# Attention's matmuls in one array tiling of 64x32 tiles, with two score buffers: four transformer layers on one core

## The chip, the core and the metric

The kernel runs on one core of a Trainium2 chip. Its engines work in parallel, each with its own queue of instructions, and wait for each other through semaphores: PE (TensorE, matrix products; its weight loads are shown apart as PEld), DVE (VectorE), ACT (ScalarE), POOL (GpSimd) and SP (SyncE, which here only issues DMAs). Matrix products go from SBUF into PSUM, whose eight banks of 128 partitions x 2 KB (512 float32 values a partition) are read by DVE and ACT. The metric is the device time of one execution in microseconds, the median of several runs.

## The reference

Four layers in a row on x of 2048 rows by 512 columns, A, B, A, B; each is `x = x + layer(layernorm(x))`. Both have 32 heads of 16 columns.

```python
def A(x, wqkv, wo):
    q, k, v = split_heads(x @ wqkv)
    p = softmax(einsum("bhqd,bhkd->bhqk", q, k) * Dh ** -0.5)
    return merge(einsum("bhqk,bhkd->bhqd", p, v)) @ wo
...
def B(x, wqkv, w_phi, wo):
    q, k, v = split_heads(x @ wqkv)
    pq, pk = q @ w_phi, k @ w_phi
    phi_q = concat(softmax(pq), softmax(-pq))
    phi_k = concat(softmax(pk), softmax(-pk))
    num = phi_q @ (phi_k.T @ v)
    den = phi_q @ sum(phi_k) + 1e-6
    return merge(num / den) @ wo
```

## The kernel before

**The softmax attention of a layer A** is one loop of 512 steps (`attention`, line 1005). Heads go in octets `o` of eight, octets in two groups `g` of four heads; a step is one (g, j, kt): four heads, a block `j` of 512 queries and a tile `kt` of 128 keys. In a step:

- `scores` (line 911) makes two score tiles ("halves") of 128 keys x 2 heads x 512 queries, each in a buffer of two PSUM banks, one head a bank. An operand has 49 rows: 16 of the high part and 32 of the low parts of float16 pairs, one of them the row of the shift. Two heads lie at partitions 0 and 64, so a half is two matmuls in row tiles of 64 (printed 49*128 in the trace). ACT reads both banks of a half at once with one exponential (line 919, 128x1024) into a float32 tile `p`.
- `pvs` (line 922) multiplies the `p` of two steps earlier (`LAG = 2`) with the values: four heads in four column tiles of 32 (128*32), each over all 128 keys, summed over the 16 tiles `kt` in one PSUM bank, tag "PV". Float32 operands take two passes. At `kt == 15` the bank holds the numerators and denominators of one block of queries; `norm` (line 533) transposes it with DVE into a tile `yt` and divides. A *turn* is the change of this accumulator, every 16 steps, 32 times a layer.
- then *pieces* of side work: projections of the next octet's q and k (`project`, line 677) and values (`values`, line 686), squares and norms, and, late in the layer, the output projection (`o_block`, line 572). A piece of a projection is `mm_cols` (line 613): four matmuls in column tiles of 32. Twelve pieces make a 128x512 result in a PSUM bank of tag "M". DVE then evacuates it: three operations for q and k (lines 792 to 794: scale and clamp from PSUM, round to float16, remainder), a transpose for values, from which 16 small DMAs on SP's queue carry the tile `vyt` to its place, one scale-and-add for the output projection (line 605). `yt`, `vyt` and `tq` share a tag of three buffers.

What orders it: PE's order is the written one (`manual_schedule` for PE), scores of both halves, PV, pieces; the other engines are ordered by the scheduler. Pieces are dealt by a credit that grows 1.33 to 1.55 a step, by a table of rates; one to three pieces a step, at least two at a turn:

```python
credit = min(credit + rate(n), 6)
least = 2 if turn else 0
most = 3
```

PSUM's eight banks are three score buffers of two banks (`psS`), and one bank each for tags "PV" and "M" (`ps1`). Outside attention the two lone banks alternate, and the three doubles serve projections, transposes and layer B. Layer B (`feed`, line 1090, and `finish`) runs block by block after the attention, with its key-value sums in one double buffer throughout. `p` tiles have six buffers.

## Time and profile before

| | us |
|---|---|
| median of the runs | 2531.31 (2529.28 to 2533.78) |
| span of the profiled execution | 2531.0 |
| first softmax attention, from its first to its last exponential | 72.5 to 1023.0 |
| second softmax attention | 1331.0 to 2279.5 |
| PE busy | 2431.7 (96%) |
| ACT busy | 2172.7 (86%), of which 1888.0 in the 2048 exponentials of line 919 |
| DVE busy | 976.1 (39%) |
| POOL busy | 381.8 (15%) |

One execution is profiled, and its instructions are grouped by line, engine, operation and tile. In a row of a group, `x2048` counts instructions, then follow their busy time in us and the mean ns of one, and behind the bar the idle time of the engine just ahead of them with the instruction that ended most of it. `49*128` or `128*32` behind a matmul is the tile of the array that it uses (rows x columns). In a row of the timeline the first number is the start in us from the span's start, the second the time until the last of the run of like instructions ends; `[0.84 <-PE s L916]` is the idle time ahead of them and what ended it. Matmul ends are modelled, so times are taken from start to start where that can be done. The granted PE clock was 1.00 in both attentions.

### The profile page before, as it was taken

The page shows a single profiled execution, that of the slowest core. Times are in us where ns is not written, and L with a number is a line of the kernel's source. Part 1 is how long each engine was busy: PE and PEld are TensorE (multiplying, and loading weights), DVE is VectorE, ACT ScalarE, POOL GpSimd, SP SyncE. Part 2 cuts the span into 40 slices and gives each one's busy share as a digit, 9 for nine tenths or more (in the row PEclk, how much of TensorE's full clock was granted, in tenths as well). Part 3 has the DMA queues.
Part 4 walks back from the last instruction along what each step waited for, and adds up shares of the span by engine and source line. Part 5 has one row for each costly group of instructions (what it writes and reads, how often), then busy time and mean ns, then how long its engine had stood idle before and what let it go on. Part 6 is the DMA issues. An engine that isn't in the chain of part 4 may idle for free.

```text
span 2531.0 us, 51504 instructions
## 1 busy us (share of the span) xinstructions
PE 2431.7 (96%) x21346; PEld 749.7 (30%) x21346; DVE 976.1 (39%) x1900; ACT 2172.7 (86%) x2429; POOL 381.8 (15%) x507
## 2 busy tenths in 40 slices
PE   6999999999999999989799999999999999998998
PEld 4222222222232222444352222222222222224543
DVE  8112211212233316989860121112122111458897
ACT  6899999999999999454439999999999999993553
POOL 3001000001000000456430010000010000005552
PEclk9999999999999999999899999999999999999999
DMA  5400320141035412101133003202300351110003
GB/s 196 73 22 6 55 40 2 27 57 58 1 80 145 161 51 76 51 9 34 59 104 49 10 10 50 37 1 47 65 1 14 68 144 38 67 68 26 10 17 110
DMA packets 110846, 135.35 MB, mean 53 GB/s; under 512 B 64024, under 2 KB 65672, under 8 KB 108424
## 3 DMA queue, kind: packets, MB, share of 16 engines
q1 hardware_dynamic: 109416, 129.18, 20.4%
q8 instruction: 169, 2.77, 0.5%
q0 software_dynamic: 1184, 2.77, 0.3%
q14 instruction: 77, 0.63, 0.1%
HBM read 60.06 MB, written 39.85 MB: 39 GB/s over the span
## 4 chain that ended last, share of the span: by engine, by line
PE 77%; DVE 12%; ACT 5%; issue 3%; POOL 2%; DMA 0%; ACTq 0%; POOLq 0%; DVEq 0%; SPq 0%
PE pv L930 37%; PE s L916 21%; PE pqk L617 6%; PE po L617 5%; ACT p L919 3%; DVE su L1173 1%; PE pbv L1103 1%; PE pk L1103 1%; PE pq L1103 1%; DVE f L1165 1%; DVE f L1166 1%; DVE mx L1162 1%; POOL f L1182 1%; DVE st L421 1%; PE pst L478 1%
## 5 line engine op out<-in xcount | busy, mean ns | idle before, releaser
L919 ACT ACTIVATE p<-s 128x1024 f32<-128x1024 f32 x2048 | 1888.0, 1115 | 14.7 <-PE s L916 11.9
L930 PE MATMUL pv<-p,v 128*32 128x512 f32 x8192 | 1093.4, 606 | 2.6 <-DVE yt L535 1.8
L916 PE MATMUL s<-kq 49*128 49x512 f16 x3872 | 607.2, 383 | 11.0 <-DMA kq<-sh 3.4
L916 PEld LDWEIGHTS <-kq 49*128 49x128 f16 x3968 | 138.3, 94 | 632.2 <-issue 620.8
L930 PEld LDWEIGHTS pv<-p,v 128*32 128x32 f32 x8192 | 162.0, 108 | 396.1 <-issue 366.1
L719 POOL TENSOR_TENSOR sq<-stg 128x512 bf16<-128x512 f16 x48 | 69.8, 1455 | 1041.5 <-DVE stg L793 938.5
L535 DVE STREAM_TRANSPOSE yt<-pv 128x512 f32<-128x512 f32 x64 | 45.8, 716 | 453.0 <-PE pv L930 436.4
L792 DVE TENSOR_SCALAR tq<-pqk,c_qk 128x512 f32<-128x512 f32 x48 | 36.0, 749 | 445.1 <-PE pqk L617 445.1
L1182 POOL TENSOR_TENSOR f<-f,su 128x1024 f32<-128x1024 f32 x62 | 119.9, 1934 | 384.6 <-DVE su L1176 352.4
L1103 PEld LDWEIGHTS <-xnTa 128*128 128x128 f16 x1152 | 110.7, 99 | 151.6 <-DVE f L1166 23.6
L617 PEld LDWEIGHTS <-wA 128*32 128x32 f16 (+1 forms) x2496 | 86.0, 97 | 196.7 <-issue 169.3
L605 DVE SCALAR_TENSOR_TENSOR xt<-po,c_oA,xt 128x512 f32<-128x512 f32 x64 | 47.1, 735 | 234.6 <-PE po L617 234.6
L617 PE MATMUL pqk<-xnTb,wA 128*32 128x512 f16 (+1 forms) x1248 | 118.7, 381 | 2.2 <-ACT xnTb L488 2.2
L617 PE MATMUL pqk<-xnT,wA 128*32 128x512 f16 (+1 forms) x1224 | 110.9, 379 | 1.2 <-ACT xnT L488 1.2
L1167 ACT ACTIVATE f<-f,c_pB 128x1024 f32<-128x1024 f32 x64 | 72.7, 1148 | 45.3 <-DVE f L1166 45.2
L1103 PE MATMUL pbv<-wbv,xnTa 128*128 128x512 f16 x384 | 92.9, 394 | 19.0 <-DVE f L1166 19.0
L1188 ACT ACTIVATE fk<-f 128x1024 f16<-128x1024 f32 x30 | 31.7, 1057 | 72.2 <-POOL f L1182 72.2
L617 PE MATMUL po<-woA,ob 128*32 128x512 f16 x1152 | 92.3, 379 | 0.0
L1103 PE MATMUL pq<-wbqk,xnTa 128*128 128x512 f16 x384 | 88.4, 379 | 0.7 <-DVE vt L1130 0.7
L1103 PE MATMUL pk<-wbqk,xnTa 128*128 128x512 f16 x384 | 88.5, 379 | 0.0
L1173 DVE TENSOR_REDUCE su<-f 128x64 f32<-128x1024 f32 x64 | 77.5, 1211 | 9.1 <-ACT f L1167 8.3
L1214 ACT ACTIVATE qT<-pqt 128x512 f32<-128x512 f32 x64 | 34.9, 593 | 49.6 <-PE pqt L1213 49.6
(283 smaller groups left out, 1895.2 us busy)
## 6 DMA issues: line engine op xcount, KB each, us to landing
kq<-stg SPq DMA_DIRECT2D x168, 128.0 KB
xd<-xt SPq DMA_DIRECT2D x40, 512.0 KB
xt<-xd SPq DMA_DIRECT2D x40, 512.0 KB
v<-vyt SPq DMA_DIRECT2D x384, 16.0 KB
oD<-osp SPq DMA_DIRECT2D x24, 256.0 KB
ob<-oD SPq DMA_DIRECT2D x8, 768.0 KB
xt<-in_A_x_dram SPq DMA_DIRECT2D x8, 512.0 KB
wbqk<-dBqk SPq DMA_DIRECT2D x2, 2048.0 KB
```

The lines of the kernel that those rows point to most:

```text
L535: nc.vector.transpose(yt.rearrange("p a b -> p (a b)"), ps)
L605: nc.vector.scalar_tensor_tensor(xt[:, u, :], ps, co, xt[:, u, :], op0=ALU.mult, op1=ALU.add)
L617: nc.tensor.matmul(ps[r, :], w[:, r], x, start=(n == 0), stop=(n == of - 1), skip_group_check=cols)
L719: nc.gpsimd.tensor_tensor(sq, hi, hi, ALU.mult)
L792: nc.vector.tensor_scalar(tq, ps, cqk, CLAMP, op0=ALU.mult, op1=ALU.min)
L916: nc.tensor.matmul(s[:, u, :], self.side(g, half, r, 0, kt * P, P), self.side(g, half, r, 1, j * 512, 512), start=True, stop=True)
L919: nc.scalar.activation(pt, s, AF.Exp, scale=0.25 / (QS * QS))
L930: nc.tensor.matmul(acc[32 * hh:32 * hh + 32, :], self.oct[o]["v"][:, r:r + 32], pt[:, hh % 2, :], start=(kt == 0), stop=(kt == NT - 1), sk ...
L1103: nc.tensor.matmul(dst, xnT[:, a, c, t * P:(t + 1) * P], w(b, c), start=(i == 0 and c == 0), stop=(i == 2 and c == NC4 - 1))
L1167: nc.scalar.activation(f, f, AF.Exp, scale=con["pB"])
L1173: nc.vector.tensor_reduce(su, f[:, r, :], AX.X, ALU.add)
L1182: nc.gpsimd.tensor_tensor(f3, f3, self.part_sums(f3, slice(0, 64), factor), ALU.mult)
```

## The change

All of attention's matmuls use tiles of 64 rows x 32 columns, so that the tiling of the array never changes inside the loop.

- *Scores*: a half is eight matmuls (four column tiles of 32 keys x two heads) in place of two.
- *PV*: for each head two matmuls, over keys 0 to 63 and 64 to 127, into two banks, which is a double buffer (`double`) of its own pool. The two banks are added later.
- *Projections*: `mm_cols` splits the contraction of 128 into halves that go to two banks (`psum_pair`), eight matmuls a piece; the norms' matmuls likewise.
- *Sums of the halves*: for PV and values DVE transposes both banks and POOL adds the two results (`turned_sum`); q and k are evacuated by five DVE operations in place of three; the output projection by two scale-and-adds.
- *PSUM*: two score buffers in place of three; one double for PV; two lone banks of tag "M" in place of "PV" and "M". Outside attention `banks` gives the two score buffers and the double in turn; layer B's key-value sums take the double.
- *Order*: scores of half 0, PV, scores of half 1, pieces. In a step whose PV opens a new accumulator (`turn`, now the step after the last product with the old one) PV comes behind the pieces; the least of two pieces is now in that step.
- The tail's output projection after attention (`cols` only while `state["att"]`) uses the whole array.

```diff
-    psS = pool("psS", bufs=3, space=bass.MemoryType.PSUM)
-    ps1 = pool("ps1", bufs=1, space=bass.MemoryType.PSUM)
+    psS = pool("psS", bufs=2, space=bass.MemoryType.PSUM)
+    psW = pool("psW", bufs=1, space=bass.MemoryType.PSUM)
+    ps1 = pool("ps1", bufs=2, space=bass.MemoryType.PSUM)
...
+    def psum_pair(name):
+        return [psum1(name + str(i)) for i in range(2)]
+    def double():
+        return psW.tile([P, 2, 512], F32, tag="W", name="double")
+    def banks(name):
+        if state["whole"]:
+            state["turn"] = (state["turn"] + 1) % 3
+            if state["turn"] == 0:
+                return double()
+        return psS.tile([P, 2, 512], F32, tag="S", name=name)
...
+    def turned_sum(ps, name):
+        ys = [np_.tile([P, 16, 32], F32, tag="yt", name=name + str(i), bufs=3) for i in range(2)]
+        for y, half in zip(ys, ps):
+            nc.vector.transpose(y.rearrange("p a b -> p (a b)"), half)
+        nc.gpsimd.tensor_tensor(ys[0], ys[0], ys[1], ALU.add)
+        return ys[0]
...
-        yt = np_.tile([P, 16, 32], F32, tag="yt", name="yt", bufs=3)
-        nc.vector.transpose(yt.rearrange("p a b -> p (a b)"), ps)
+        yt = turned_sum(ps, "yt")
...
-                    nc.vector.scalar_tensor_tensor(xt[:, u, :], ps, co, xt[:, u, :], op0=ALU.mult, op1=ALU.add)
+                    for half in ps if cols else (ps,):
+                        nc.vector.scalar_tensor_tensor(xt[:, u, :], half, co, xt[:, u, :], op0=ALU.mult, op1=ALU.add)
...
+        for i in range(4):
+            c = slice(32 * i, 32 * i + 32)
+            for h in range(2):
+                r = slice(64 * h, 64 * h + 64)
+                nc.tensor.matmul(ps[h][c, :], w[r, c], x[r], start=(n == 0), stop=(n == of - 1), skip_group_check=True)
...
-                    nc.vector.tensor_scalar(tq, ps, cqk, CLAMP, op0=ALU.mult, op1=ALU.min)
-                    nc.vector.tensor_scalar(hi, tq, -CLAMP, None, op0=ALU.max)
-                    nc.vector.scalar_tensor_tensor(lo, tq, -CLAMP, hi, op0=ALU.max, op1=ALU.subtract)
+                    nc.vector.tensor_scalar(tq, ps[0], cqk, None, op0=ALU.mult)
+                    nc.vector.scalar_tensor_tensor(tq, ps[1], cqk, tq, op0=ALU.mult, op1=ALU.add)
+                    nc.vector.tensor_scalar(tq, tq, CLAMP, -CLAMP, op0=ALU.min, op1=ALU.max)
+                    nc.vector.tensor_copy(hi, tq)
+                    nc.vector.tensor_tensor(lo, tq, hi, ALU.subtract)
...
+            s = psS.tile([P, 2, 512], F32, tag="S", name="s")
+            for c in range(4):
                 for u in range(2):
...
+                    nc.tensor.matmul(s[32 * c:32 * c + 32, u, :], self.side(g, half, 64 * u, 0, kt * P + 32 * c, 32),
+                                     self.side(g, half, 64 * u, 1, j * 512, 512), start=True, stop=True, skip_group_check=True)
...
-                self.acc = ps1.tile([P, 512], F32, tag="PV", name="pv")
+                pair = double()
+                self.acc = [pair[:, h, :] for h in range(2)]
...
+                for h in range(2):
+                    r = slice(64 * h, 64 * h + 64)
+                    nc.tensor.matmul(acc[h][32 * hh:32 * hh + 32, :], self.oct[o]["v"][r, x:x + 32],
+                                     pt[r, hh % 2, :], start=(kt == 0), stop=(kt == NT - 1), skip_group_check=True)
...
-                    self.scores(g, j, kt)
+                    self.scores(g, j, kt, 0)
                     pend.append((g, j, kt))
-                    turn = False
-                    if len(pend) > LAG:
-                        turn = pend[0][2] == NT - 1
+                    turn = len(pend) > LAG and pend[0][2] == 0
+                    if len(pend) > LAG and not turn:
                         self.pvs(*pend.popleft())
+                    self.scores(g, j, kt, 1)
...
+                    if turn:
+                        self.pvs(*pend.popleft())
```

How instructions move shows at three places. The first is PE in a plain step of the first attention, between the scores of a step's second half and a piece. Names such as `kq_1_981` are tiles with a running number, `kq_0` and `kq_1` the operands of the two halves, `wA` the weights of a projection. Before:

```order
L916 LDWEIGHTS kq_1_981
L916 MATMUL s<-kq_1_981 128x512
L930 MATMUL pv<-p,v_157 32x512 x4
L617 LDWEIGHTS wA
L617 MATMUL pqk<-xnT_3_152,wA 32x512
```

And now, where the scores of half 0 end and those of half 1 begin:

```order
L944 LDWEIGHTS kq_0_593
L944 MATMUL s<-kq_0_593 32x512
L961 MATMUL double<-p,v_160 32x512 x8
L944 LDWEIGHTS kq_1_594
L944 MATMUL s<-kq_1_594 32x512
```

PV, now eight matmuls, has moved from behind both halves to between them, and a score matmul writes 32 keys in place of 128.

The second is PE at a turn of the new kernel: the end of a piece of the values' projection (two banks, `pv_2268` and `pv_2269`), the first PV on the new accumulator, and the next step's first scores.

```order
L642 LDWEIGHTS wAv
L642 MATMUL pv_2268<-xnT_3_155,wAv 32x512
L642 LDWEIGHTS wAv
L642 MATMUL pv_2269<-xnT_3_155,wAv 32x512
L961 MATMUL double<-p,v_160 32x512 x8
L944 LDWEIGHTS kq_0_593
L944 MATMUL s<-kq_0_593 32x512
```

Here PV stands behind the pieces and directly ahead of the next step's scores of half 0.

The third is DVE around a turn in the second octet: an evacuation of q or k (`pqk`) and then `norm` of a finished accumulator. Before:

```order
L792 TENSOR_SCALAR tq<-pqk,c_qk 128x512
L793 TENSOR_SCALAR stg<-tq 128x512
L794 SCALAR_TENSOR_TENSOR stg<-tq,stg 128x512
L535 STREAM_TRANSPOSE yt<-pv 128x512
L537 TENSOR_SCALAR rec<-yt 128x16
L538 RECIPROCAL rec<-rec 128x16
L542 TENSOR_TENSOR yn<-yt,rec 128x16x16
```

And now:

```order
L819 TENSOR_SCALAR tq<-pqk_4630,c_qk 128x512
L820 SCALAR_TENSOR_TENSOR tq<-pqk_4631,c_qk,tq 128x512
L821 TENSOR_SCALAR tq<-tq 128x512
L822 CAST stg<-tq 128x512
L823 TENSOR_TENSOR stg<-tq,stg 128x512
L548 STREAM_TRANSPOSE yt_5174<-double 128x512
L548 STREAM_TRANSPOSE yt_5175<-double 128x512
L555 TENSOR_SCALAR rec<-yt_5174 128x16
L556 RECIPROCAL rec<-rec 128x16
L560 TENSOR_TENSOR yn<-yt_5174,rec 128x16x16
```

Five operations stand ahead of two transposes where three stood ahead of one; between the second transpose and the division POOL's `L549 TENSOR_TENSOR yt_5174<-yt_5174,yt_5175 128x512` makes the sum.

More of the change, by code (lines that the diff above doesn't have):

```diff
@@ L585, in o_block @@
             if wide:
-                ps2 = psS.tile([P, 2, 512], F32, tag="S", name="po2")
+                ps2 = banks("po2")
             if early and t2 == 0:
@@ L629, in v_block @@
         for t2 in range(2):
-            ps = psS.tile([P, 2, 512], F32, tag="S", name="pv_")
+            ps = banks("pv_")
             for u in range(2):
@@ L695, in values @@
                         yield
-            yt = np_.tile([P, 16, 32], F32, tag="yt", name="vyt", bufs=3)
-            nc.vector.transpose(yt.rearrange("p a b -> p (a b)"), ps)
+            yt = turned_sum(ps, "vyt")
             for a in range(4):
@@ L859, in feed_end @@
         def feed_end(self):
-            ps = psS.tile([P, 2, 512], F32, tag="S", name="pqk2")[:, 0, :]
+            ps = banks("pqk2")[:, 0, :]
             run(self.project(0, NJ - 1, ps, 0))
@@ L1092, in feed @@
             if self.kvp is None:
-                self.kvp = psS.tile([P, 2, 512], F32, tag="S", name="kvp")
+                self.kvp = double()
+                state["whole"] = False
             qT = [big([P, 4, 512], F32, f"qT{j}_{i}") for i in range(2)]
@@ L1240, in heads @@
             for k in range(2):
-                ps = [psS.tile([P, 2, 512], F32, tag="S", name="pn") for _ in range(2)]
+                ps = [banks("pn") for _ in range(2)]
                 for g in range(4):
```

75 lines of the change are left out of this document (34 added, 41 removed).

## The prediction

> **What bounds the kernel now.** First the share of each engine by stage (busy time of line 919 alone in four stretches: us, busy us and count, clock, DMA share, GB/s), then the page's groups and its chain, then the timeline of single steps.
>
> ```profile
> core 0: us, ACT busy (x), PEclk, DMA share, GB/s
> 72.50:1023.00 950.50, 944.72 (x1024) 1.00 0.24 56
> 400.00:600.00 200.00, 199.68 (x218) 1.00 0.22 40
> 1331.00:2279.50 948.50, 943.25 (x1024) 1.00 0.20 45
> ```
>
> The first and third stretch are the two softmax attentions: 1899 of the span's 2531.0 us, and each runs 1024 exponentials (two a step, 512 steps). In a quiet stretch 218 of them take 199.68 us: **0.917 us each, 1.83 us a step**. At that cadence one attention lasts 1024 × 0.917 = 939 us; it takes 950.5 and 948.5. So ACT stands still, or gets its scores late, for only 11.5 + 9.5 = 21 us in all. That is all that a faster TensorE could win.
>
> ```profile
> PE 77%; DVE 12%; ACT 5%; issue 3%; POOL 2%; DMA 0%; ACTq 0%; POOLq 0%; DVEq 0%; SPq 0%
> L919 ACT ACTIVATE p<-s 128x1024 f32<-128x1024 f32 x2048 | 1888.0, 1115 | 14.7 <-PE s L916 11.9
> 400.00:600.00 200.00, 199.45 (x1896) 48.19 (x1888) 40.36 (x80) 199.68 (x218) 13.14 (x11) 1.00 0.22 40
> ```
>
> The chain (first row) names PE, which reads as if PE alone set the pace. The last row (PE, PEld, DVE, ACT, POOL busy in 400 to 600 us) shows PE and ACT both full: the side work is dealt out at 1.33 to 1.55 pieces a step, so that PE's step comes out as long as ACT's. One step of PE:
>
> ```profile
> 599.71 0.61 PE L916 MATMUL s<-kq 49*128 49x512 f16 x4
> 600.25 1.07 PE L930 MATMUL pv<-p,v 128*32 128x512 f32 x8
> 601.13 0.61 PE L617 MATMUL pqk<-xnT,wA 128*32 128x512 f16 x8
> 601.67 0.60 PE L916 MATMUL s<-kq 49*128 49x512 f16 x4
> 602.21 1.07 PE L930 MATMUL pv<-p,v 128*32 128x512 f32 x8
> 603.09 0.40 PE L617 MATMUL pqk<-xnT,wA 128*32 128x512 f16 x4
> 603.42 0.61 PE L916 MATMUL s<-kq 49*128 49x512 f16 x4
> ```
>
> From start to start: two side pieces and the way back to the scores 0.54 us, one piece and the way back 0.33, so a piece is 0.215 and the way back 0.11. PV takes 0.88. Scores (two groups of 0.215) and the way to PV take 0.54, again 0.11 over. The shapes beside the times say what the 0.11 is: 49*128 to 128*32 and back, the two changes of tiling in a step.
>
> **The change part by part.** *One tiling.* It removes 2 × 0.11 = 0.22 us a step from PE: 1.96 becomes 1.74 with two pieces, some 1.61 on the mean. Over 1024 steps PE loses 225 us of work; ACT's cadence hides all but the 21 us. The Trainium skill, TensorEngine Tiling (Array Packing), Key Properties, has it that a change of tiling mode drains TensorE; the rows agree, at 0.11 us. The same page, PSUM Bottleneck, warns that tiling speeds up TensorE and not the reading of PSUM; by it nothing but those 21 us could come of this, and the rows say the same.
>
> *Twice the matmuls.* Groups become 8 tiles of 64x32, each with half of the rows. That two row halves run at once is in the pairs of 49*128 above, four column tiles in 128*32; both together only another stage shows, with 16 tiles of 32*32 (the first two rows are what starts within 0.1 us, the third what starts within 2.5 us):
>
> ```profile
> 1199.11 0.19 PEld L1246 LDWEIGHTS pn<-qT,kvb 32*32 32x32 f32 x21 [1.23 <-ACT kvb L1232]
> 1199.11 0.69 PE L1246 MATMUL pn<-qT,kvb 32*32 32x512 f32 x12 [0.32 <-ACT kvb L1232]
> 1199.11 1.14 PE L1246 MATMUL pn<-qT,kvb 32*32 32x512 f32 x28 [0.32 <-ACT kvb L1232]
> q8 instruction: 169, 2.77, 0.5%
> ```
>
> 28 passes take 1.14 us where PV's 8 passes take 1.07: the tiles overlap. 33 instructions start in 0.1 us, 3 ns each, so 8 tiles start within some 0.05 us; a group lasts as long as before and its last tile ends 0.05 later. The Trainium skill, TensorEngine Tiling (Array Packing), Instruction Overhead, gives each matmul about 60 cycles and warns of small pieces; if those were spent one after the other, the burst above could not be, so the trace speaks against it here. The burst was queued, though. Over a whole attention PE now takes 64 instructions a step for scores and PV (loads, and PV's second pass, counted) and 16 for a piece, 86 at 1.4 pieces, one per 21 ns; before it was 24 and 8, so 35, one per 52; the instruction queue (last row) then has to bring twice as many of its 16 KB packets. That is a rival below.
>
> *Two score buffers.* PE's queue in a plain step is now: scores of half 0, PV, scores of half 1, pieces. I count from the moment (0) at which ACT ends the exponential that frees half 0's buffer; the next ends are due at 0.917, 1.833, 2.75.
>
> ```profile
> 620.53 0.61 PE L916 MATMUL s<-kq 49*128 49x512 f16 x4
> 621.02 1.02 ACT L919 ACTIVATE p<-s 128x1024 f32<-128x1024 f32 x1
> 1331.97 1.93 ACT L919 ACTIVATE p<-s 128x1024 f32<-128x1024 f32 x2
> 1333.95 0.61 PE L916 MATMUL s<-kq 49*128 49x512 f16 x2 [0.26 <-ACT p L919]
> ```
>
> From scores to their exponential 0.49 us (620.53 to 621.02), which then takes 1.02 when it has not been queued behind another; from ACT's end (1331.97 + 1.93 = 1333.90) to waiting scores 0.05. So: scores 0.05, PV 0.27 to 1.15, second scores at 1.15 (their buffer was free at 0.97), exponential ends by 1.15 + 0.49 + 0.05 + 1.02 = 2.71, due 2.75. Two pieces bring PE back at 1.15 + 0.215 + 0.43 = 1.79, before 1.83 when the next buffer comes free. **A plain step just holds ACT's cadence, with 0.04 us to spare**; a step of three pieces (103 in the new order) is 0.13 late on its first half and less on its second. That eats about what the lost mode changes give, save at places named below.
>
> *The turn.* Every 16 steps the accumulator changes. Now both banks are one buffer, DVE must empty both, and the new order puts PV behind the pieces, with no PV between the two score groups. Of the 64 turns 21 have one piece ahead of PV, 27 two, 4 three, 5 a float32 transpose of about 1 us, the rest none (counted in the order of instructions).
>
> ```profile
> 105.03 1.07 PE L930 MATMUL pv<-p,v 128*32 128x512 f32 x8
> 106.16 0.72 DVE L535 STREAM_TRANSPOSE yt<-pv 128x512 f32<-128x512 f32 x1 [13.84 <-PE pv L930]
> 106.99 0.16 PEld L930 LDWEIGHTS pv<-p,v 128*32 128x32 f32 x8 [0.42 <-DVE yt L535]
> ```
>
> From the last PV's start to the transpose 1.13, the transpose 0.72, so two of them 1.44 and 0.05 to PE. In the turn's step: scores 0.05, second scores 0.97 to 1.18, one piece to 1.40, PV to 2.28, and only then the next step's scores: their exponential ends at 2.28 + 0.49 + 0.05 + 1.02 = 3.84, due 3.67, 0.17 late. After them PV again to 3.38 and second scores: 3.38 + 1.56 = 4.94, due 0.917 after 3.84, 0.18 more. **A turn costs 0.35 us with one piece, 0.56 with two, 0.79 with three, 1.2 with a transpose:** 21 × 0.35 + 27 × 0.56 + 4 × 0.79 + 5 × 1.2 = 32 us. What is late next is every later exponential, since ACT has no slack to catch up. DVE, in the same count, ends both transposes near 1.06 if it starts at once; PV wants the banks at 1.40 or 1.61, so 0.34 to 0.55 us of other DVE work ahead of them is free, and more is not.
>
> *DVE, POOL and the yt buffers.*
>
> ```profile
> L535 DVE STREAM_TRANSPOSE yt<-pv 128x512 f32<-128x512 f32 x64 | 45.8, 716 | 453.0 <-PE pv L930 436.4
> L792 DVE TENSOR_SCALAR tq<-pqk,c_qk 128x512 f32<-128x512 f32 x48 | 36.0, 749 | 445.1 <-PE pqk L617 445.1
> L793 DVE TENSOR_SCALAR stg<-tq 128x512 f16<-128x512 f32 x48 | 20.4, 425 | 1.6
> L794 DVE SCALAR_TENSOR_TENSOR stg<-tq,stg 128x512 f16<-128x512 f32 x48 | 34.4, 716 | 1.5
> L605 DVE SCALAR_TENSOR_TENSOR xt<-po,c_oA,xt 128x512 f32<-128x512 f32 x64 | 47.1, 735 | 234.6 <-PE po L617 234.6
> L719 POOL TENSOR_TENSOR sq<-stg 128x512 bf16<-128x512 f16 x48 | 69.8, 1455 | 1041.5 <-DVE stg L793 938.5
> L1182 POOL TENSOR_TENSOR f<-f,su 128x1024 f32<-128x1024 f32 x62 | 119.9, 1934 | 384.6 <-DVE su L1176 352.4
> 72.50:1023.00 950.50, 947.09 (x8744) 237.90 (x8744) 241.46 (x534) 944.72 (x1024) 40.60 (x39) 1.00 0.24 56
> L701 SPq DMA_DIRECT2D v<-vyt x384: 585/599/1906, 102.9 to 1806.6; - x192
> ```
>
> A projection's evacuation grows from 0.749 + 0.425 + 0.716 = 1.89 us to about 3.0 (five operations, the two that read PSUM by 0.749 and 0.735, the others by 0.43 to 0.72): 48 × 1.15 = 55 us more. 64 turns and 24 value pieces add 88 transposes of 0.716, 63 us; the output projection's second addition 64 × 0.735 = 47. Of 165 us most falls into the attentions, where DVE is busy 241.46 of 950.5 us: hidden, unless it comes just ahead of a turn. The POOL addition has no row of its shape: half of line 1182's 1.934 is 0.97, line 719 has 1.455 for as many elements; I take 1.2, between them. DVE's next instruction in order waits for it. At a turn that comes after the transposes, so PV isn't held by it; but if a value piece's sum or an evacuation stands right before, the transposes come 1 to 3 us late, where 0.4 is free. And yt has three buffers, which a value piece holds until 16 small transfers land (last row, 0.6 us each on one queue, some 10 us); the new order reuses 8 of 24 after 8 to 9.5 steps, 15 to 18 us, the others later, so this holds in the mean. I put 8 us on all this: 8 meetings of 1 us. Bounds: 0 if none meets, and 62 × 1 + 24 × 2 = 110 if all do.
>
> *Relief.* Of the 21 us some doesn't go away:
>
> ```profile
> 78.90 1.94 ACT L919 ACTIVATE p<-s 128x1024 f32<-128x1024 f32 x2 [0.84 <-PE s L916]
> 1337.92 1.94 ACT L919 ACTIVATE p<-s 128x1024 f32<-128x1024 f32 x2 [1.27 <-PE s L916]
> 698.20 1.94 ACT L919 ACTIVATE p<-s 128x1024 f32<-128x1024 f32 x2 [0.67 <-PE s L916]
> ```
>
> At the two starts (rows one and two) ACT waits for the first operands, some 5 us; around 690 to 756 us (row three) full-size float32 transposes lie between scores, some 4 us. The other 12 are stalls of 0.1 to 0.2 us behind steps of two or three pieces; the three-piece steps keep a third of them, so I take −8, bounds 0 and −16.
>
> *Outside attention* the same three pairs of banks turn in order, and lone banks of tag M stay two; only layer B's accumulator now has the double buffer and leaves two to the rest, as it left two of three before. The last turns and the drain at the end have a second transpose and the sum with no cover: 2 × (0.72 + 1.2) with the waits behind it, +3.
>
> **Sum** against the profiled execution's span of 2531.0, which is also the median of the runs (2531.31) within 0.3: + 32 − 8 + 8 + 3 = + 35, so **2566 us**; with the turn at two thirds and the bounds on the relief and DVE kept small, 2548 to 2595.
>
> **Rivals.** *Faster:* the 1.02 of an exponential that wasn't queued holds 0.1 us which the cadence of 0.917 overlaps; if a late one costs only what PE is late, a turn with one piece costs 0.07 + 0.08 and one with two 0.28 + 0.08, and if the second half catches up too, almost nothing for the first kind. Then 64 turns are some 6 us, the relief is 16: 2531 − 10 = 2521. For it: 14.7 us is all that ACT now idles before line 919 by the profile. Against it: the moment of the next scores, 2.28 or later, hangs on PV's 0.88, which is well measured. The other side of the forecast, 0.16. *No change:* turns at half (16), relief 12, rest nothing: within 5 us of 2531, 0.10. *Round trip too long:* if the 8 tiles of a PV take 0.95 instead of 0.88, or the way from scores to ACT 0.57, the 0.04 of slack is gone and each second half is late by some 0.05; at 1024 steps 51 us on top of the forecast, 2617, at double that 2668. It decides from 0.04 us a step on. 0.09. *DVE and the yt buffers hold PE* at most turns, the 110 in place of the 8: 2668, by halves 2617; 0.05. *The feed of PE or the tiles fail:* at 52 ns an instruction a step takes 86 × 0.052 = 4.5 us in place of 1.83, and 1024 steps take 2700 us longer; row halves that ran one after the other would double scores and PV (+1.3 us a step). The burst of 33 in 0.1 us and the 49*128 pairs speak against both; 0.03.
>
> **How the numbers follow.** Forecast 0.57, faster 0.16, no change 0.10, round trip 0.09, DVE 0.05, feed 0.03. About 0.2%, 5 us, is what a measurement of this kernel can tell from no change. Faster 0.16, within 0.2% 0.10, slower 0.57 + 0.09 + 0.05 + 0.03 = 0.74. The range 2514 to 2635 takes in the forecast, the faster case and the lower halves of the round trip and of DVE; left out are their upper halves, the feed and the edge of the faster case, about 0.13.
>
> **What would show it.** No 0.11 between groups of PE, a step of 1.74 with two pieces, and PE waiting for ACT at the first scores of plain steps: the tiling works. ACT's ends 0.917 apart in plain steps, and gaps of 0.15 to 0.4 us in the two or three exponentials behind every sixteenth step: the turn. Idle DVE at the turns: no hold there. It is wrong if ACT's gaps come in every step (the round trip), if PE's instructions start 50 ns apart (the feed), if PE waits at the turn for line 548's transposes by more than 0.5 us (DVE), or if no gap stands at the turns at all.

## The result and the profile after

| | before | changed |
|---|---|---|
| median of the runs, us | 2532.4 (2529.28 to 2533.78) | 2681.73 (2680.33 to 2685.0) |
| span of the profiled execution, us | 2531.0 | 2683.2 |
| first attention, first to last exponential, us | 950.1 | 1039.5 |
| second attention, us | 948.3 | 1003.2 |

(The median before is now that of four runs; 2531.31 above was that of three.) The kernel became 5.9% slower: ratio 1.059, 95% interval 1.0575 to 1.0605. Of the 152.2 us between the two profiled executions 89.4 lie in the first attention, 54.9 in the second and 8 outside. The changed kernel's page, engines, chain and the costliest groups, and ACT's exponential in the two attentions (us, busy us and count, clock of PE):

```profile
PE 2365.4 (88%) x46698; PEld 1097.1 (41%) x46698; DVE 1134.5 (42%) x2153; ACT 2188.2 (82%) x2428; POOL 494.7 (18%) x595
ACT 43%; PE 17%; DVE 16%; issue 12%; SPq 5%; POOL 4%; DMA 2%; ACTq 0%; DVEq 0%; POOLq 0%
L947 ACT ACTIVATE p<-s 128x1024 f32<-128x1024 f32 x2048 | 1904.4, 1056 | 142.0 <-PE s L944 136.2
L961 PE MATMUL double<-p,v 64*32 64x512 f32 x16384 | 1118.7, 601 | 29.2 <-DVE yt L548 28.8
```

```profile
72.50:1112.10 1039.60, 953.09 (x1024) 0.97 0.23 53
1426.70:2430.00 1003.30, 951.35 (x1024) 0.98 0.20 44
```

PE is busy for less (2365 us for 2432; since the ends of matmuls are modelled, the 225 us of the count can't be read off this), and ACT now idles 142 us ahead of its exponentials where it idled 14.7. The granted clock, 1.00 in both attentions before, is 0.97 and 0.98. The rest of the loss is found by the ends of the exponentials. At ACT's cadence they are 0.917 us apart; what an end comes later than that is called lost time here. The table sorts it by place; the five steps around each turn are put down to that turn.

| lost by ACT in both attentions, us | before | changed |
|---|---|---|
| steps away from turns | 10.3 | 27.5 |
| turns whose longest single stall is below 0.9 us | 7.3 in 62 | 23.2 in 41 |
| turns with a longer stall ("held") | 3.5 in 2 | 114.5 in 23 |
| all | 21 | 165 |

**Plain steps** are what the change was made for. The timeline of PE and ACT in a quiet stretch of the changed kernel:

```profile
599.30 6.56 ACT L947 ACTIVATE p<-s 128x1024 f32<-128x1024 f32 x7
...
600.57 0.41 PE L944 MATMUL s<-kq 49*32 49x512 f16 x8
600.78 0.63 PE L642 MATMUL pqk<-xnT,wA 64*32 64x512 f16 x16
601.32 0.41 PE L944 MATMUL s<-kq 49*32 49x512 f16 x8
601.54 1.05 PE L961 MATMUL double<-p,v 64*32 64x512 f32 x16
602.40 0.41 PE L944 MATMUL s<-kq 49*32 49x512 f16 x8
```

From group to group there is no 0.11 left: scores 0.21, two pieces 0.54 with the wait for the buffer, PV 0.86. Seven exponentials run without a gap on two buffers.

**An undisturbed turn** (step 35 of the first attention):

```profile
137.14 1.31 DVE L548 STREAM_TRANSPOSE yt<-double 128x512 f32<-128x512 f32 x2 [9.29 <-PE double L961]
...
138.50 0.41 PE L944 MATMUL s<-kq 49*32 49x512 f16 x8 [0.51 <-ACT p L947]
138.72 0.63 PE L642 MATMUL pv<-xnT,wAv 64*32 64x512 f16 x16
139.15 1.05 PE L961 MATMUL double<-p,v 64*32 64x512 f32 x16
140.01 0.41 PE L944 MATMUL s<-kq 49*32 49x512 f16 x8
140.23 1.05 PE L961 MATMUL double<-p,v 64*32 64x512 f32 x16
...
140.55 5.77 ACT L947 ACTIVATE p<-s 128x1024 f32<-128x1024 f32 x6 [0.26 <-PE s L944]
```

Scores, two pieces, PV, and only then the next scores, at 140.01; ACT has been idle for 0.26 us when their exponential starts. The end comes 0.37 late, the second half's another 0.16. DVE had both transposes done at 138.45, in time.

**A held turn** (step 275, the longest): what DVE, SP, PE and ACT do.

```profile
607.10 12.61 SPq L725 DMA_DIRECT2D v<-vyt  x16
619.81 0.54 SPq L154 DMA_DIRECT2D awo<-in_A_wo_dram  x1
...
625.59 2.46 DVE L325 TENSOR_REDUCE pk<-awo 128x1 f32<-128x512 f32 x4 [17.19 <-DMA awo<-in_A_wo_dram]
...
629.70 1.30 DVE L548 STREAM_TRANSPOSE yt<-double 128x512 f32<-128x512 f32 x2
...
619.00 0.41 PE L642 MATMUL pqk<-xnT,wA 64*32 64x512 f16 x8
631.06 1.96 PE L961 MATMUL double<-p,v 64*32 64x512 f32 x16 [11.64 <-DVE yt L548]
632.76 0.68 PE L944 MATMUL s<-kq 49*32 49x512 f16 x8
633.19 1.96 PE L961 MATMUL double<-p,v 64*32 64x512 f32 x16
...
633.55 1.02 ACT L947 ACTIVATE p<-s 128x1024 f32<-128x1024 f32 x1 [12.98 <-PE s L944]
635.68 1.94 ACT L947 ACTIVATE p<-s 128x1024 f32<-128x1024 f32 x2 [1.11 <-PE s L944]
```

DVE's order is fixed, and in it the reductions of a weight load stand ahead of the accumulator's transposes. SP issues that load at 619.81, behind sixteen transfers of a value sum; DVE waits 17.19 us for it; PE waits 11.64 us for DVE; the next scores stand behind PV, so ACT waits 12.98.

The kernel before has the same queue on SP and no such wait:

```profile
577.05 0.54 SPq L143 DMA_DIRECT2D awo<-in_A_wo_dram  x1
L314 DVE TENSOR_REDUCE pk<-awo x4: 675/676/678, 596.2 to 598.0; 128x1 f32<-128x512 f32 x4
```

There too the load comes right behind sixteen transfers of a value sum. But in DVE's order the transpose of this turn and two evacuations stand between, and the reductions start 19 us after the load's issue. In neither attention does DVE wait there for a weight load. So this hold is no old wait that the third score buffer had covered: DVE's order, which the scheduler makes for each program, came out another.

After the hold PV takes 1.70 us to the next scores (631.06 to 632.76) where it takes 0.86. The clock of PE around it (us, PE busy and count, clock):

```profile
619.00:631.00 12.00, 0.41 (x16) 0.68 0.61 199
631.00:632.00 1.00, 0.94 (x16) 0.50 0.00 0
635.00:636.00 1.00, 1.00 (x32) 0.50 0.00 0
637.00:639.00 2.00, 1.81 (x56) 1.00 0.03 8
```

The granted clock is 0.50 for nearly six us of work after the pause. This is seen behind twelve of the stalls: the second half that follows ends 1.2 us late each time (1.22 here, with 1.11 of it as ACT's idle time), where it is 0.16 late in the undisturbed turn above.

What the 23 held turns (and the step beside them at 415) waited for, by the instruction that DVE, POOL or PE stood at in the trace. This sorting is a reading; the experiments test some of its rows. ("The yt round" is the sharing of the three `yt` buffers among norms, evacuations and value sums.)

| cause | turns (step; second attention marked 2) | us lost |
|---|---|---|
| the yt round: buffers that a value sum holds | 131, 147, 2:19, 2:147 | 33.7 |
| DVE in front of a weight load | 275, 403 (and 7.5 at step 415) | 27.4 |
| pieces at the turn that wait for an evacuation or a norm's square | 195, 291, 323, 451, 2:179 | 17.9 |
| DVE in the layer norm of the next layer | 2:467, 2:483, 2:499 | 15.1 |
| POOL's reduction of an octet's bound, and DVE behind it | 115, 227 | 9.8 |
| first turns and five of 1 to 2 us | 3, 243, 339, 371, 387, 2:3, 2:163 | 10.9 |

DVE's waits over both attentions, by what ended them (us in all, times, longest):

```profile
DVE rec L555 <- POOL yt L549: 97.1, 60, 6.9
...
DVE yt L548 <- DMA v<-vyt: 21.1, 4, 10.9
DVE pk L325 <- DMA awo<-in_A_wo_dram: 17.2, 1, 17.2
DVE pk L325 <- DMA bwv<-in_B_wqkv_dram: 15.3, 1, 15.3
DVE pk L325 <- DMA bwo<-in_B_wo_dram: 11.4, 2, 6.3
```

The longest in the second row, 10.9, held nothing: it ended at 1936.5, by when PE had only just ended its last product with the old accumulator. The longest that held a turn there is 8.5 us, at step 2:147.

### The profile page after: what moved, and what is told of

It is laid out like the page before. It is cut to its first block, busy times and chain, and to the rows that moved or that the text cites. A ratio compares the mean times of both kernels' runs of the same rounds, so it can differ in the third digit from the quotient of the medians.

```text
span 2683.2 us, 102802 instructions
## 1 busy us (share of the span) xinstructions
PE 2365.4 (88%) x46698; PEld 1097.1 (41%) x46698; DVE 1134.5 (42%) x2153; ACT 2188.2 (82%) x2428; POOL 494.7 (18%) x595
## 4 chain that ended last, share of the span: by engine, by line
ACT 43%; PE 17%; DVE 16%; issue 12%; SPq 5%; POOL 4%; DMA 2%; ACTq 0%; DVEq 0%; POOLq 0%
ACT p L947 42%; PE double L961 5%; PE s L944 3%; SPq L725 3%; DVE su L1207 1%; PE pbv L1137 1%; PE po L636 1%; PE pk L1137 1%; DVE xt L625 1%; DVE yt L548 1%; PE pq L1137 1%; POOL f L1216 1%; POOL yt L549 1%; DVE st L432 1%; PE pqk L642 1%
## 5 line engine op out<-in xcount | busy, mean ns | idle before, releaser
L961 PE MATMUL double<-p,v 64*32 64x512 f32 x16384 | 1118.7, 601 | 29.2 <-DVE yt L548 28.8
L944 PE MATMUL s<-kq 49*32 49x512 f16 x15488 | 829.8, 385 | 135.6 <-ACT p L947 98.1
L944 PEld LDWEIGHTS <-kq 49*32 49x32 f16 x15872 | 385.2, 90 | 923.7 <-issue 841.3
L961 PEld LDWEIGHTS double<-p,v 64*32 64x32 f32 x16384 | 318.1, 107 | 109.2 <-DVE yt L548 32.7
L549 POOL TENSOR_TENSOR yt<-yt,yt 128x512 f32<-128x512 f32 x64 | 81.7, 1276 | 958.5 <-DVE yt L548 874.1
L548 DVE STREAM_TRANSPOSE yt<-double 128x512 f32<-128x512 f32 x128 | 84.4, 695 | 379.5 <-PE double L961 357.7
L642 PE MATMUL po<-woA,ob 64*32 64x512 f16 x2304 | 102.9, 380 | 15.7 <-DVE sBv_es L136 8.3
L642 PE MATMUL pqk<-xnT,wA 64*32 64x512 f16 x2304 | 102.1, 377 | 9.0 <-DVE vyt L548 7.1
L642 PE MATMUL pqk<-xnTb,wA 64*32 64x512 f16 x2304 | 98.5, 376 | 0.0
L642 PEld LDWEIGHTS <-wA 64*32 64x32 f16 x4608 | 76.0, 93 | 52.0 <-issue 21.8
```

Of the source, the lines that this page charges most:

```text
L548: nc.vector.transpose(y.rearrange("p a b -> p (a b)"), half)
L549: nc.gpsimd.tensor_tensor(ys[0], ys[0], ys[1], ALU.add)
L642: nc.tensor.matmul(ps[h][c, :], w[r, c], x[r], start=(n == 0), stop=(n == of - 1), skip_group_check=True)
L944: nc.tensor.matmul(s[32 * c:32 * c + 32, u, :], self.side(g, half, 64 * u, 0, kt * P + 32 * c, 32), self.side(g, half, 64 * u, 1, j * 512, ...
L961: nc.tensor.matmul(acc[h][32 * hh:32 * hh + 32, :], self.oct[o]["v"][r, x:x + 32], pt[r, hh % 2, :], start=(kt == 0), stop=(kt == NT - 1), ...
```

## The experiments

Medians; the kernel before ran beside them at 2531.2 to 2532.4. "Lost" is ACT's time lost in both attentions, counted as above (changed kernel: 165).

**Two buffers in the old order** (one timed execution).

```diff
-    psS = pool("psS", bufs=3, space=bass.MemoryType.PSUM)
+    psS = pool("psS", bufs=2, space=bass.MemoryType.PSUM)
```

> The kernel before with two score buffers in place of three, nothing else. If the changed kernel can live with two buffers only because of its new order (scores, PV, scores, pieces) and because no change of tiling stands in the step, the old order must be far slower here: second scores wait for ACT until 0.97 us, then 0.215 + 0.11 + PV 0.88 + 0.11 + 1.4 pieces x 0.215 until the next step's first scores at some 2.6 us in place of 1.83; 1024 steps x 0.75 = +770 us, some 3300 us. Rival: two buffers cost about the same in any order (the third was worth little): below 2700 us.

2954.6 us; lost 267. Theory and rival were both wrong on the size: the third buffer is worth 246 us in the attentions, a third of my count, and some 176 outside them. Of the 267 us only 9 lie in held turns (four of them, the longest stall 2.2 us).

**The new order in the old tilings** (one timed execution): the same two buffers, scores, PV, scores, pieces.

```diff
-                    self.scores(g, j, kt)
+                    self.scores(g, j, kt, 0)
                     pend.append((g, j, kt))
...
                         self.pvs(*pend.popleft())
+                    self.scores(g, j, kt, 1)
```

> The kernel before with two score buffers and the order scores, PV, scores, pieces in every step, in the old tilings, PV's accumulator in one bank. By the prediction's count a change of tiling of 0.11 stands ahead of PV and behind it: second scores at 1.37 us, their exponential 0.13 late; with two pieces the next first scores 0.36 late, with one 0.14. 1024 steps x some 0.25 = 250 us in the attentions, beside what two pairs of banks cost outside them (some 170 us, as in the run with two buffers in the old order): 2950 us, ACT's lost time in the attentions about 270 us. Rival (the order alone makes two buffers enough): lost time in the attentions below 100 us.

2912.8 us; lost 223, of which 148 in plain steps: near the theory (2950 and 270), and the rival is out. One of its steps, PE and ACT:

```profile
599.96 0.39 PE L916 MATMUL s<-kq 49*128 49x512 f16 x2
600.28 1.06 PE L930 MATMUL pv<-p,v 128*32 128x512 f32 x8
601.27 0.39 PE L916 MATMUL s<-kq 49*128 49x512 f16 x2
...
601.79 3.89 ACT L919 ACTIVATE p<-s 128x1024 f32<-128x1024 f32 x4 [0.27 <-PE s L916]
```

Scores 0.32 and PV 0.99 to the next group, each with a change of tiling of 0.11 in it, and ACT 0.27 late. So one tiling does what it says: with two buffers plain steps lose 148 us without it and 27 with it. The run shows one thing more: with two score buffers, but the old accumulator of one bank and the old evacuations, there are 3 held turns with 8 us (the longest stall 1.5), and PE waits at most 0.8 us for a turn's transpose. So the loss of the third score buffer does not make the long holds by itself; they come with what else the change brought to DVE.

**PV in its plain place at a turn.**

```diff
-                    if len(pend) > LAG and not turn:
+                    if len(pend) > LAG:
...
-                    if turn:
-                        self.pvs(*pend.popleft())
```

> The changed kernel with PV in its plain place at a turn too (between the two score groups). Theory (DVE late, PE held): by the count of the prediction PV then waits for both transposes until some 1.1 us, ends near 2.0, the second scores' exponential is 0.8 us late in place of 0.53, and what holds DVE holds PE just as long: 2690 to 2710 us. Rival (the long stalls come from the pieces that now stand ahead of PV at a turn): the 23 long stalls shrink, 2600 to 2640 us.

2696.65 us (ratio 1.0652, 1.0634 to 1.0669); lost 178. An undisturbed turn costs 0.75 to 0.9 in place of 0.53, and the held ones cost 111 us, as the theory had it. That PV was put behind the pieces is not the cause; with pieces at a turn it is the better of these two places.

**A buffer of its own for the value sum**: tag "vh" with one buffer, two for yt.

```diff
-        ys = [np_.tile([P, 16, 32], F32, tag="yt", name=name + str(i), bufs=3) for i in range(2)]
+        tags = ("vh", 1) if name == "vyt" else ("yt", 2), ("yt", 2)
+        ys = [np_.tile([P, 16, 32], F32, tag=t, name=name + str(i), bufs=n) for i, (t, n) in enumerate(tags)]
```

> The changed kernel, with the value sum that waits for 16 small transfers in a buffer of its own and the other users of the yt tag in two: no more memory. Theory (the round of three buffers that a value sum blocks for 10 us is what holds DVE at 4 of the 23 long stalls, steps 131 and 147 of the first layer, 19 and 147 of the second, 34 us with what follows them): 2645 to 2660 us, and those four stalls gone. Rival (DVE and SP are late there anyway): within 8 us of 2682.

2713.46 us (1.0715, 1.0697 to 1.0733), slower by 32. The stalls at 147 and 2:147 went, but 131 hardly shrank, 2:19 grew to 9.8, and new ones of 6.9, 10.1 and 13.4 us came at 19, 141 and 2:144; lost 191. DVE's waits say why:

```profile
DVE vyt L549 <- DMA v<-vyt: 68.9, 7, 15.8
```

Seven value sums now wait for the one before. Its transfers are not done after the 10 us that they take, since SP's queue gets to them late; one buffer is not enough for that queue.

**Two weight loads by POOL's queue**, and landing steps 9 for 5 elsewhere.

```diff
-        wo = load_w(a_wo, "awo")
+        wo = load_w(a_wo, "awo", q=nc.gpsimd)
...
-        wv = load_w(b_wqkv[:, 1024:1536], "bwv")
+        wv = load_w(b_wqkv[:, 1024:1536], "bwv", q=nc.gpsimd)
```

> The changed kernel with two weight loads (awo, bwv) issued by POOL's queue in place of SP's, and more steps between the other loads and their use. Theory (at steps 275, 403 and 415 DVE stands 17, 15 and 11 us in front of loads that SP issues late, with the accumulator's transposes queued behind; 15 + 12 + 7 us with what follows): 2645 to 2660 us, those three stalls gone. Rival (PE would be held there by the next thing in line): 2670 us or more.

2676.74 us (1.0575, 1.0557 to 1.0593), lost 150: by its median not told apart from the changed kernel. The stalls at 275 and 403 went (27 us), and others of 8.4, 3.3, 4.2 and 4.1 came at 396, 408, 419 and 499, as the rival had it. DVE still stands before these loads, 10.9 and 9.3 us, at other moments. So no run shows what the weight loads are worth by themselves.

**A chain of four, each with one edit more.** First the two halves of a value sum in an xt buffer:

```diff
+        if name == "vyt":
+            pair = xp.tile([P, 2, 16, 32], F32, tag="xt", name=name)
+            ys = [pair[:, i] for i in range(2)]
```

> First of four kernels that each add one edit. Here the two halves of a value sum go into one of the three xt buffers, which stand empty while values are projected, so yt serves norms and evacuations alone. Theory (the round of three yt buffers, with two taken by each sum, holds DVE; a single buffer for it only made the next value sum wait, 69 us over 7 waits): no DVE wait on the transfers of vyt is left, the stalls at 131, 147 and 19, 147 go, 34 us: 2645 us (2638 to 2655). Rival (SP's queue is late whatever the buffers, and the hold moves elsewhere): above 2665 us.

2659.67 us (1.051, 1.0492 to 1.0527), 22 us less, between the theory's range and the rival's; lost 141. The stalls at 147 and 2:147 are gone, 131 and 2:19 fell from 12.9 to 6.2 together. No DVE wait for the transfers of vyt is left. The yt round is shown as a cause, for 22 us of the 33.7.

Second, the sum of an accumulator's halves on DVE:

```diff
-        nc.gpsimd.tensor_tensor(ys[0], ys[0], ys[1], ALU.add)
+        (nc.gpsimd if name == "vyt" else nc.vector).tensor_tensor(ys[0], ys[0], ys[1], ALU.add)
```

> As the first, and the sum of an accumulator's two halves made by DVE in place of POOL. DVE now waits 1.3 to 1.5 us for POOL's sum at each of some 60 turns and does nothing meanwhile; its own sum should take 0.7. Theory (what stands behind that wait on DVE, an evacuation or a second addition, is what PE's pieces wait for at turns such as 195, 179 and 451): 5 to 15 us less than the first kernel. Rival (nothing that PE needs stands behind it): within 3 us of the first.

2647.18 us (1.0444, 1.0414 to 1.0473), 12 us less, as the theory had it, though its runs spread over 17 us; lost 135. DVE's own sum takes 0.69 us, where it had waited 1.3 to 1.5 for POOL's.

Third, `landing` 9 for 5, and the output weights asked for at step 358 in place of 348:

> As the second, and eight steps more between the weight loads and DVE's first operation on them (the output weights of layer A are then asked for ten steps later). Theory (DVE stands 17, 15 and 11 us before loads, 34 us with what follows): 20 to 34 us less than the second kernel, no DVE wait on awo, bwv and bwo above 3 us. Rival: as in the run with POOL's queue, other holds take their place: less than 8 us gained.

2649.88 us (1.0469, 1.0451 to 1.0486), lost 127: nothing by the median, as the rival had it. DVE's waits for the loads:

```profile
DVE pk L325 <- DMA awo<-in_A_wo_dram: 17.1, 1, 17.1
...
DVE pk L325 <- DMA bwv<-in_B_wqkv_dram: 6.1, 1, 6.1
```

The wait for awo is as long as in the changed kernel (17.2): the place in the program moved, DVE still came to it 17 us early. The wait for bwv fell from 15.3 to 6.1, and the lost time hardly.

Fourth, no pieces in the step of a turn, rates 0.05 higher:

```diff
-                        if n < self.hold and not turn:
+                        if n < self.hold or turn:
                             break
```

> As the third, and no pieces in the step that opens a new accumulator (the rates are 0.05 a step higher, so that they are done in other steps). By the count of the prediction PV then ends at 2.06 us, the next first scores are in time, only the second ones 0.14 late: a turn costs 0.15 in place of 0.53, 64 x 0.4 = 25 us, and pieces that wait for DVE no longer stand ahead of PV at a turn: 25 to 40 us less than the third kernel. Rival (the pieces are only moved, and steps of three pieces or pieces held by DVE cost the same elsewhere): less than 10 us.

2602.51 us (1.0274, 1.0252 to 1.0295), 47 us less, more than the 25 to 40 expected, the largest step and the best kernel of this family; lost 85: 28 in plain steps, 13 in 53 undisturbed turns (0.25 each, most of them 0.10 or 0.21, counted 0.15), 43 in 11 held ones. Its turn at step 35:

```profile
135.01 9.44 ACT L951 ACTIVATE p<-s 128x1024 f32<-128x1024 f32 x10
...
136.15 0.41 PE L948 MATMUL s<-kq 49*32 49x512 f16 x8 [0.51 <-ACT p L951]
136.37 1.05 PE L965 MATMUL double<-p,v 64*32 64x512 f32 x16
137.22 0.41 PE L948 MATMUL s<-kq 49*32 49x512 f16 x8
137.44 1.05 PE L965 MATMUL double<-p,v 64*32 64x512 f32 x16
```

PV directly behind the second scores, the next scores 0.85 behind it, and ten exponentials without a gap.

**The same edit alone**, on the changed kernel:

> The changed kernel with one edit: no pieces in the step that opens a new accumulator (rates 0.05 a step higher). In the chain this edit came fourth and took 47 us off. Theory (what makes turns expensive is the order scores, scores, pieces, PV: the 0.53 of an undisturbed turn, 64 x 0.4 = 25 us, and pieces that wait for DVE with PV and the next scores behind them, some 20 us): 2630 to 2650 us by itself. Rival (the yt round has to be mended first, since it holds the transposes too): above 2660 us.

2637.34 us (1.0423, 1.0406 to 1.0441), 44 us less, as the theory had it; lost 118: 24 in plain steps, 15 in 47 undisturbed turns, 79 in 17 held ones. Pieces at a turn cost 44 us by themselves and 47 in the chain. Not all of this is the order alone: DVE's waits for awo and bwv also fell, from 17.2 and 15.3 to 6.8 and 7.6, and the hold at 275 from 15 to 3 us. The yt round still holds at 147, 2:19 and 2:147 (10.5, 9.6, 11.5).

**Second scores ahead of PV in the step behind a turn**, on the chain without its third edit:

```diff
+                    next_ = len(pend) > LAG and pend[0][2] == 1
-                    if len(pend) > LAG and not turn:
+                    if len(pend) > LAG and not turn and not next_:
                         self.pvs(*pend.popleft())
                     self.scores(g, j, kt, 1)
+                    if next_:
+                        self.pvs(*pend.popleft())
```

> Values in xt, sum on DVE, no pieces at a turn (as the fourth kernel of the chain, without its later use of the loads), and in the step behind a turn the second scores ahead of PV. By the count of the prediction the second scores of that step are then issued as soon as ACT frees their buffer (2.80 us), their exponential is in time, and PV from 3.01 to 3.89 delays the next first scores by nothing: an undisturbed turn costs nothing in place of 0.2, 50 turns x 0.2 = 10 us: 2590 to 2597 us. Rival (ACT's lost time at turns comes from the transposes that DVE ends late, whatever the order behind): within 4 us of 2602.

2618.58 us (1.0332, 1.0315 to 1.0349), 16 us slower than the fourth of the chain; an undisturbed turn costs 0.69. Neither theory nor rival holds: my count had left out that step's pieces, which now stand between PV and the next first scores.

```profile
138.93 1.05 PE L965 MATMUL double<-p,v 64*32 64x512 f32 x16
139.79 0.63 PE L646 MATMUL pv<-xnT,wAv 64*32 64x512 f16 x16
140.22 0.41 PE L948 MATMUL s<-kq 49*32 49x512 f16 x8
```

**Pieces as before, scores and PV in one tiling**: one bank each, two in turn, the old evacuations.

```diff
-            for h in range(2):
-                r = slice(64 * h, 64 * h + 64)
-                nc.tensor.matmul(ps[h][c, :], w[r, c], x[r], start=(n == 0), stop=(n == of - 1), skip_group_check=True)
+            nc.tensor.matmul(ps[c, :], w[:, c], x, start=(n == 0), stop=(n == of - 1), skip_group_check=True)
...
-                    ps = psum_pair("pqk")
+                    ps = psum1("pqk")
```

> The changed kernel with the pieces of side work as before: 128x32 tiles, one bank each, so that the two M banks take turns and evacuation has three operations again; scores and PV stay in 64x32 tiles. Theory (the pair of M banks is what pieces wait for at turns): stalls such as 131, 179, 195 and 451 vanish, 40 to 60 us; but two changes of tiling of 0.11 come back in steps with pieces, and a step with two of them is 0.13 late, 400 steps x 0.2 = 80 us: 2700 us, with plain steps' lost time near 100 us and held turns' near 60. Rival (changes of tiling are hidden behind ACT): 2620 to 2640 us.

2643.18 us (1.0454, 1.0432 to 1.0476), 39 us less than the changed kernel, near the rival. Lost 129: held turns 48 in 12, undisturbed 42 (0.80 each, since two changes of tiling lie in a turn), plain steps 39, not 100. So one tiling for the pieces buys 11 us in plain steps and 0.2 to 0.3 at a turn, and in the changed kernel it costs more, by what comes with it at held turns (pairs of banks, five operations for three, two yt buffers a value sum for one; the run does not split these). **Without pieces at a turn, and the accumulator's sum on DVE**:

> As the run with pieces in the old tiling, no pieces at a turn, and the sum of the accumulator's halves on DVE. Theory: another 45 us less than that run, as in the chain. Rival (with two M banks in turn pieces no longer wait at turns, so only the 25 us of an undisturbed turn are left to win): 20 to 30 us less.

2644.17 us (1.0442, 1.0425 to 1.046), nothing gained, so neither theory nor rival; lost 130. Undisturbed turns fell to 0.56, but stalls of 5 to 10 us came up at 323, 387, 2:19 and 2:211. **With values in xt and the second scores first behind a turn**:

> The run with pieces in the old tiling and none at a turn, with values in xt and the second scores ahead of PV behind a turn. Theory (its long stalls at 147, 19 and 211 are the yt round, 26 us; the order behind a turn another 10 to 20): 2600 to 2612 us, still slower than before, since the changes of tiling around pieces keep plain steps' lost time near 40 us. Rival (DVE's order holds PE elsewhere instead): above 2625 us.

2652.17 us (1.0472, 1.0454 to 1.0489), above 2625 as the rival had it: the holds fell from 53 to 37 us, and undisturbed turns doubled to 1.0, for the reason of the run above.

This run and the one with the second scores ahead of PV behind a turn (2618.58) differ in the pieces' tiling alone, with the banks and evacuations that go with it; there the one tiling is 34 us ahead. So the 39 us against it are a figure for the changed kernel, with its pieces at the turns, its yt round and POOL's sum, and not for the tiling as such.

No version beat the kernel before; the lowest is 2602.5.

## Why the prediction was wrong

The forecast was +35 us, to 2566; it became +152 by the profiled executions. Point by point:

- *What bounds the kernel*: right. ACT's cadence of 0.917 holds in quiet stretches of the changed kernel, and less work for PE won nothing.
- *One tiling, twice the matmuls, two buffers in a plain step*: right. Eight tiles run at once (PV's sixteen matmuls take 0.86 us where eight took 0.88), no 0.11 is left between groups, and the step keeps the cadence; without one tiling plain steps with two buffers lose 148 us.
- *The turn*: right in mechanism and size, 0.53 with two pieces where 0.56 was counted. 64 undisturbed turns at the mean of 0.57 would be 36 us, counted 32. Taking the pieces out of it brought 44 us, of which some 16 are this term (64 turns at 0.32 in place of 0.57) and the rest holds.
- *DVE, POOL and the yt buffers*: **the term that failed.** I put 8 us, "8 meetings of 1 us"; 23 turns were held, for 114.5 us, of which 13 are their undisturbed price: 101 in place of 8. The rival of this name gave 2668 at a chance of 0.05. That its sum comes near is partly luck: it added up 62 meetings of 1 us and 24 of 2, and what came was 23 holds of 1 to 15 us. Three things were mis-sized. The length of a hold was taken from DVE's own work (1 to 3 us), but DVE waits in order for others: 17, 15 and 11 us for weight loads, which the term had at nothing, and up to 8.5 for the yt round where it held. The trace before has no wait for weight loads; they came with DVE's new order, so the place to look for them was the order of the changed program. The 10 us of a value sum's transfers were set against 15 to 18 us until the buffer's reuse, "so this holds in the mean"; SP's queue comes late to them, and this round cost 33.7 us, 22 of them taken away by xt buffers; ahead of the hold at step 131 the queue of the changed kernel has eleven us of other transfers (the last of them shown) before the sixteen of the value sum:

```profile
308.35 5.02 SPq L930 DMA_DIRECT2D kq<-sh  x6
313.49 11.56 SPq L725 DMA_DIRECT2D v<-vyt  x16
```

 And behind a long hold PE runs at half clock, which no term had: 12 times some 1.0 us more on the next half alone (1.2 for 0.16), and up to 0.84 on PV itself (1.70 for 0.86).
- Nor was it counted that pieces at a turn have PV and the next scores queued behind them, so that a piece that waits for an evacuation or a norm's square (17.9 us in five turns) holds all of it. Before, PE had no such wait in the first attention. PE's wait for DVE's transposes in the first attention (us in all, times, longest), before and, in the second row apart, changed:

```profile
PE pv L930 <- DVE yt L535: 0.8, 2, 0.6
```

```profile
PE double L961 <- DVE yt L548: 18.4, 5, 11.6
```

- *Relief*: −8 was expected, plain steps lost 17 more: 7.5 of it the hold at step 415, the rest mostly stalls of 0.3 to 0.7 us, which I lay to norms and float32 transposes without the third buffer's cover; that is not shown one by one.
- *Outside attention*: 8 us where 3 were counted.

What is not settled: why DVE comes to awo so early in its new order, 17 us before the load in the changed kernel and with eight steps more between them; and the split of the remaining 85 us of the best kernel, of which 43 are holds. The third score buffer is not what kept the holds away, since two buffers in the old tilings have 8 to 9 us of them. Nor had the kernel before a spare accumulator: it too had one bank, and PE waited for its transpose, but never over 0.6 us. Which part of the change makes the holds (two banks to empty at a turn, longer evacuations, two yt buffers a sum, or DVE's order around them) is split only as far as the experiments go. A kernel with a spare accumulator would need two banks more than the eight, and was not tried.

## What to carry to other kernels

When a change gives an in-order engine more work ahead of a moment that another engine needs, read the new program's order: list what stands ahead of that moment, with what each instruction there waits for, and take the longest wait and not the mean length of the work. The old trace does not show all of them: the wait of 17 us was not in it. Look at the queues that fill those waits (here one DMA queue with 384 small transfers) before trusting a transfer's own time. Split a uniform change into its parts: with two buffers, scores and PV in one tiling saved plain steps some 110 us (148 to 39 lost); the pieces in the same tiling cost 39 us in the changed kernel and gained 34 in the kernel without pieces at the turns. A part's price holds for the kernel in which it was measured.

## What was not expected of the hardware

- PE's granted clock falls to 0.50 around a pause, and stays there for some 3 to 6 us of full work: after 12.0, 7.5 and 3.75 us of pause (steps 275, 149 and 131), after 2.85 (step 115) and after two pauses of 0.6 and 1.6 close together (step 195), not after one of 2.2 (step 293). So the length of a pause alone does not decide. In the trace's record of the clock the 15 stretches at 0.50 in the two attentions last 3.41 us or a multiple of it; the longest, at step 275, goes from 623.21 to 636.86. The Trainium skill, TensorE: Matmul & The Clock Gate, What's actually happening, has half rate after an idle window of about 3.4 us and full rate after as much sustained work; the runs agree in size, though less than 3.4 us of pause was already enough.
- PE's order in the first attention, 21,440 matmuls and as many loads where there were 8,744, met no limit of instruction feed: in quiet stretches some 84 instructions a step start within 1.83 us, one per 22 ns.
